# V in bursts of 1, 8, 5, 3 and 1 key tiles, double score tiles, and a new order of a head pair's steps

## The chip, the cores and the metric

One core of one Trainium2 chip runs the kernel. Its engines are TensorE (PE; its weight loads are listed as PEld), VectorE (DVE), ScalarE (ACT), GpSimd (POOL) and SyncE (SP, which here only issues DMAs). The metric is the device time of one execution in microseconds (us), less is better. Engines take their instructions in the order in which the program issues them and wait for each other by semaphores.

## The reference, cut to what matters

```python
def _attn_ref(q, k, v):                        # (2, 8, 1152, 64) each, q and k scaled up by 8
    q_pool = q.reshape(B, H, S // 2, 2, D).mean(axis=3)
    scores = (1 / np.sqrt(D)) * q_pool @ k.transpose(0, 1, 3, 2)
    scores = scores - scores.max(-1, keepdims=True)
    attn = np.exp(scores)
    attn = attn / (attn.sum(-1, keepdims=True) + 1e-09)
    return attn @ v                            # (2, 8, 576, 64)

x = attn_out.transpose(0, 2, 1, 3).reshape(1152, 512)
x = mlp(x, moe_w_in, moe_w_out)                # 512 -> 2048 -> 512, h * tanh(softplus(h)) between
return mlp(x, moe2_w_in, moe2_w_out)           # the same sizes, ELU between
```

## The kernel before

**Attention.** `attention()` works on eight pairs of heads, one after the other. The two heads of a pair lie on the two halves of the 128 partitions, so that score matmuls contract 64 rows each and two run side by side (shape 64x128 in the traces). A pair has 576 pooled queries; they are cut into c=0 (256 queries) and c=1 (320). The 1152 keys are nine key tiles of 128. A pair is 18 steps (`NS`): nine key tiles for c=0, then nine for c=1.

A step's `qk` makes one score tile, keys on the partitions and queries along the row, with three products of split operands (`kh`, `kl`, `qh`, `ql`; L343) and a fourth matmul that adds the negated row maxima `tops` (L345). `exp` (L351, ScalarE) writes its exponential into `pts`. `av` (L420) multiplies a key tile of V with it and accumulates over the nine tiles; this is in full fp32 (two passes for each matmul), with the two heads on the two halves of the columns (shape 128x64). `total` (L375) sums the exponentials over the keys, in tiles of 32 columns (128x32), from the last two key tiles and two partial sums that GpSimd adds up (`add`, L364). The sums go by way of DRAM to another layout and back (`spill`, `sum_out`, `sum_in`, `invert`, `inv_out`, `inv_in`), and then `scale` (L437), `token_high` and `token_low` write the result as split tokens `XH`, `XL`.

The row maxima of the next pair come first. `peak_mm` (L273, L280) makes a rough score with queries on the partitions, `peak` reduces it on VectorE (L286, L288, L289): 13 entries, of which entry 11 is the one with the remaining queries (L280; three matmuls, two reductions, its third part in PSUM bank 6). `top`, `top_out` (L320) and `top_in` (L326, L331) bring the maxima through DRAM into the rows `tops`; the first two query tiles after entry 5 (for c=0), the rest after entry 12 (for c=1). For pair 0 they are turned by PE instead (`flip`).

**PSUM.** Score tiles, row maxima, the sum of c=0 and the flips take turns on three slots of two banks each (`take`, a ring in program order). Bank 6 holds the V accumulator of c=0, the sum of c=1 and the third part of entry 11; bank 7 the V accumulator of c=1.

**The order.** All of it is written out by hand: `at(step, list, function)` puts a call into a step's list, and the loop over steps issues, in each step, the lists `pre`, `peak`, `qk`, `exp`, `av`, `act`, `dve`, `rest`, `pool` and `sp` (`peak` stands before `qk` in odd steps and behind it in even ones). V comes in bursts of two key tiles in every second step, from step 10 of a pair to step 26. In between, one piece of an MLP weight per pair is read in two halves (`read`, `read2`), rescaled on ScalarE (`rebias`, L119), and turned to split fp32 in further steps by its age in steps. The loop ends nine steps after the last score; what is left then is issued between the blocks of the MLP (`after`).

**MLP.** `mlps()` runs two layers in 96 units, each of 12 matmuls L178 and 12 (first layer) or 9 (second) matmuls L661. The first layer's first units read tokens of batch 0; tokens of c=1 of batch 1 are first read by unit 12.

Of the kernel before, what the change touches and what calls it, by code (L numbers as in the profile page):

```python
# [22 lines left out]
def tile_pool_attention_mish_elu_mlp(  # L23
# [159 lines left out]
    def attention():  # L183
        with ExitStack() as st:
# [268 lines left out]

            last = n_pairs * NS
            WHEN = [-14, -12, -10, -9, -8, -7, -6, -4, -3, -2, 0, 1, 2]
            for n in range(n_pairs):
                s0 = n * NS
                if n:
                    for i in range(2):
                        at(s0 - 26 + 2 * i, "sp", load_q, n, slice(0, SQ), slice(i, i + 1))  # L460
                        at(s0 - 21 + 3 * i, "sp", load_k, n, slice(i * S // 2, (i + 1) * S // 2))
                        at(s0 + [-2, 4][i], "sp", load_v, n, i)
                    at(s0 - 18 if n == 1 else s0 - 20, "pool", pool_q, n, nc.gpsimd)
                    at(s0 - 15 if n == 1 else s0 - 18, "act", high_q, n)
                    at(s0 - 17, "act", high_k, n, slice(0, S // 2))
                    at(s0 - 15, "act", high_k, n, slice(S // 2, S))
                    at(s0 - 12, "act", blk_q, n)
                    at(s0 - 10, "pool", low_q, n, nc.gpsimd)
                    at(s0 - 9, "pool", low_k, n, nc.gpsimd, slice(0, S // 2))
                    at(s0 - 8, "pool", low_k, n, nc.gpsimd, slice(S // 2, S))  # L470
                    for e, r in enumerate(WHEN):
                        at(s0 + r, "peak", peak_mm, n, e)
                        at(s0 + r, "dve", peak, n, e)
                    for r, t0, t1 in (WHEN[5], 0, 2), (WHEN[12], 2, NQ):
                        at(s0 + r + 1, "sp", top_out, n, t0, t1)
                        at(s0 + r + 3, "sp", top_in, n, t0, t1)
                for c in range(2):
                    u0 = s0 + KT * c
# [4 lines left out]
                    at(t0, "av", total, n, c)  # L483
                    at(t0 + 1, "pre", spill, n, c)
                    at(t0 + 1, "sp", sum_out, n, c)
                    at(t0 + 3, "sp", sum_in, n, c)
# [57 lines left out]
            while s < last + 9:  # L544
# [16 lines left out]
                for w in list(going):  # L561
                    w.age += 1
                    f = {6: w.read2, 9: w.rebias, 10: w.clamp, 12: w.shift, 13: w.words, 14: w.high, 15 if s > last else 22: w.rest}.get(w.age)
                    if f:
                        f()
# [241 lines left out]
```

## Time and profile before

| | |
|---|---|
| time, median of 3 runs | 646.53 us (645.66 to 646.84) |
| profiled execution, its own time | 647.42 us |
| its span | 645.6 us |
| busy: PE, DVE, ACT, POOL | 97%, 65%, 52%, 35% of the span |
| PE share of the chain that ended last | 85% |
| first score of pair 1, of pair 7 | 40.0 us, 206.9 us |
| first matmul of the MLP | 239.8 us |

The chain is followed back from the last instruction, step by step, to what released it. Its PE part by line: L178 and L661 (the MLP) 31% each, L420 8%, L343 6%. Times in the views are from the span's start. A PE row's length reaches to the modelled end of its last matmul, and rows overlap; what a matmul costs in a row of its like is read from start to start.

### The profile page before, as it was taken

Reading aid. Unit: us, or ns where it says so; the run is one execution under the profiler, and the core shown is the slowest. Engines: PE = TensorE matmul, PEld = TensorE weight load, DVE = VectorE, ACT = ScalarE, POOL = GpSimd, SP = SyncE. Lnnn points to the kernel's source line nnn. Section 1 sums busy time; section 2 is a strip of 40 time slices with the busy share of each in tenths; the row PEclk is TensorE's granted clock in tenths of the full one; section 3 lists DMA queues with packets and bytes.
Section 4 is the critical chain, followed back from the end, with each engine's and each line's share of the span. In section 5 each row is a group of like instructions: output and inputs, shape, how many; then the busy total and the mean of one; then the engine's idle time right before and its main releaser. Section 6 shows DMA issues by size and latency. Waiting matters only on the chain.

```text
span 645.6 us, 11750 instructions
## 1 busy us (share of the span) xinstructions
PE 629.3 (97%) x4626; PEld 535.9 (83%) x4626; DVE 421.7 (65%) x684; ACT 336.0 (52%) x682; POOL 227.6 (35%) x216
## 2 busy tenths in 40 slices
PE   5999999999999999999999999999999999999997
PEld 3666666666666669999999999999999999989995
DVE  5656666666666339466476657877887778995453
ACT  2655645546564456334345443546776566655442
POOL 5758686675866441101013223432201011100000
PEclk9999999999999999999999999999999999999999
DMA  4243443534342334242231233221223123310111
GB/s 156 63 101 84 100 95 72 139 73 98 83 100 64 87 92 142 66 131 65 66 120 59 85 98 98 65 73 60 97 67 98 43 89 98 97 34 1 50 50 49
DMA packets 50527, 53.36 MB, mean 83 GB/s; under 512 B 17640, under 2 KB 39080, under 8 KB 50472
## 3 DMA queue, kind: packets, MB, share of 16 engines
q1 hardware_dynamic: 49960, 51.90, 28.7%
q8 instruction: 36, 0.59, 0.4%
q10 hardware_dynamic: 512, 0.72, 0.3%
q14 instruction: 19, 0.16, 0.1%
HBM read 50.14 MB, written 2.47 MB: 81 GB/s over the span
## 4 chain that ended last, share of the span: by engine, by line
PE 85%; DMA 5%; DVE 3%; SPq 3%; ACT 2%; issue 1%; POOL 0%; DVEq 0%; POOLq 0%; ACTq 0%
PE banks L178 31%; PE banks L661 31%; PE banks L420 8%; PE banks L343 6%; PE banks L273 3%; PE banks L375 3%; PE banks L345 2%; DMA top<-hopm 2%; DVE stat L288 1%; DVE stat L286 1%; DMA hopm<-neg 1%; SPq L326 1%; DMA kr<-in_k_dram 1%; ACT QH L246 1%; ACT pt L351 1%
## 5 line engine op out<-in xcount | busy, mean ns | idle before, releaser
L123 POOL TENSOR_SCALAR wf<-wf 128x512 f32<-128x512 f32 x64 | 42.8, 670 | 259.1 <-ACT wf L119 214.5
L286 DVE TENSOR_REDUCE stat<-banks 128x2 f32<-128x768 f32 x96 | 91.1, 957 | 58.9 <-PE banks L273 58.9
L178 PE MATMUL banks<-XH,wh 128*128 128x384 f32 x384 | 129.5, 337 | 0.0
L178 PE MATMUL banks<-XL,wh 128*128 128x384 f32 x384 | 129.4, 337 | 0.0
L178 PE MATMUL banks<-XH,wl 128*128 128x384 f32 x384 | 129.4, 337 | 0.0
L351 ACT ACTIVATE pt<-banks 128x512 f32<-128x512 f32 (+1 forms) x144 | 90.1, 652 | 73.4 <-PE banks L345 73.4
L420 PE MATMUL banks<-pt,vr 128*64 128x320 f32 (+1 forms) x576 | 85.1, 418 | 0.0
L178 PEld LDWEIGHTS banks<-XH,wh 128*128 128x128 f32 x384 | 72.0, 188 | 2.3 <-issue 0.5
L178 PEld LDWEIGHTS banks<-XL,wh 128*128 128x128 f32 x384 | 72.0, 188 | 1.8
L364 POOL TENSOR_TENSOR add<-add,pt 128x512 f32<-128x512 f32 (+1 forms) x48 | 67.1, 1422 | 14.4 <-ACT pt L351 13.7
L178 PEld LDWEIGHTS banks<-XH,wl 128*128 128x128 f32 x384 | 72.0, 188 | 0.0
L615 ACT ACTIVATE gh<-banks 128x384 fp32r<-128x384 f32 x48 | 23.6, 492 | 80.5 <-PE banks L178 80.4
L661 PE MATMUL banks<-gh,wl 128*128 128x384 f32 x192 | 64.5, 336 | 0.0
L661 PE MATMUL banks<-gl,wh 128*128 128x384 f32 x192 | 64.5, 336 | 0.0
L661 PE MATMUL banks<-gh,wh 128*128 128x384 f32 x192 | 64.4, 335 | 0.0
L364 POOL TENSOR_TENSOR add<-pt 128x512 f32<-128x512 f32 (+1 forms) x32 | 45.3, 1416 | 48.0 <-ACT pt L351 48.0
L420 PEld LDWEIGHTS banks<-pt,vr 128*64 128x64 f32 x576 | 35.2, 136 | 27.9 <-issue 12.9
L661 PE MATMUL banks<-wl,gh 128*128 128x512 f32 x144 | 56.2, 390 | 0.0
L661 PE MATMUL banks<-wh,gl 128*128 128x512 f32 x144 | 56.2, 390 | 0.0
L661 PE MATMUL banks<-wh,gh 128*128 128x512 f32 x144 | 56.2, 390 | 0.0
L618 DVE TENSOR_TENSOR gl<-g,gh 128x384 fp32r<-128x384 f32 x48 | 31.1, 649 | 35.2 <-ACT g L616 35.2
L343 PE MATMUL banks<-QH,KH 64*128 64x320 f32 (+1 forms) x288 | 50.3, 337 | 0.8 <-ACT pt L351 0.5
(80 smaller groups left out, 1199.7 us busy)
## 6 DMA issues: line engine op xcount, KB each, us to landing
raw<-in_moe_w_in_dram SPq DMA_DIRECT2D x28, 512.0 KB
raw<-in_moe_w_out_dram SPq DMA_DIRECT2D x28, 512.0 KB
vr<-in_v_dram SPq DMA_DIRECT2D x16, 288.0 KB
qr<-in_q_dram SPq DMA_DIRECT2D x14, 288.0 KB
kr<-in_k_dram SPq DMA_DIRECT2D x14, 288.0 KB
raw<-in_moe_w_in_dram SPq DMA_DIRECT2D x8, 256.0 KB
raw<-in_moe_w_out_dram SPq DMA_DIRECT2D x8, 256.0 KB
out_dram<-part SPq DMA_DIRECT2D x8, 256.0 KB
```

Source lines behind the costliest of these rows:

```text
L123: nc.gpsimd.tensor_scalar(self.f, self.f, HUGE, -HUGE, op0=ALU.min, op1=ALU.max)
L178: nc.tensor.matmul(pt[:, :TB], w[:, kk * P:(kk + 1) * P], x[:, kk, tk], start=(i == 0), stop=(i == len(terms) - 1))
L273: nc.tensor.matmul(pt[:, h, :KB], qh[n][half[h], t * P:(t + 1) * P], kh[n][half[h], j * KB:(j + 1) * KB], start=True, stop=True,)
L286: nc.vector.tensor_reduce(m[:, t, :, j], pt[:, :, :KB], axis=AX.X, op=ALU.max)
L343: nc.tensor.matmul(pt[:, h, :w], x[half[h], kk], y[half[h], cols], start=(i == 0), stop=False)
L351: nc.scalar.activation(pts[n, c][:, kt], sc.pop((n, c, kt))[:, :, :w], AF.Exp, scale=SCALE)
L364: nc.gpsimd.tensor_tensor(d, d if i is None else p[:, i], p[:, j], op=ALU.add)
L375: nc.tensor.matmul(pt[32 * g:32 * (g + 1), :w], ones[:, :32], x[:, h, z * w:(z + 1) * w], start=(i == 0), stop=(i == len(srcs) - 1), tile_ ...
L420: nc.tensor.matmul(acc[n, c][half[h], :w], vs[n][:, h, kt, :], pts[n, c][:, kt, h, :], start=(kt == 0), stop=(kt == KT - 1),)
L615: nc.scalar.activation(gh, h, AF.Mish)
L618: nc.vector.tensor_tensor(gl, g, gh, op=ALU.subtract)
L661: nc.tensor.matmul(pt, l, r, start=(first and i == 0), stop=(final and i == 2))
```

## The change

`qk` and `exp` take a number m of key tiles. For key tiles 0, 2 and 6 of c=0 m is 2: the step's score tile and the next one's lie side by side in one slot (256 columns of each bank each), one exponential reads both, and the next step makes none. V is multiplied at steps 9 (key tile 0 of c=0), 16 (the other eight), 22 (tiles 0 to 4 of c=1), 25 (5 to 7) and 27 (the last). A list `late` stands behind `qk` and `exp`; the row maxima have times in half steps, even ones in `peak` (now always before `qk`), odd ones in `late`. The steps of loads, casts, splits, maxima, adds, sums, their chains and the weight's parts are taken from tables, `PREP[1]` for pair 1, `PREP[2]` for pairs 2 to 7 and `PLAN` for all. Keys are loaded, cast and split in parts of 768 and 384 instead of 576 and 576. The first pair's row maxima and flips stand in other steps as well. The MLP is as before.

```diff
-            def qk(n, c, kt):
+            def qk(n, c, kt, m):
                 o, w = cut[c][0], cut[c][1] - cut[c][0]
-                pt = sc[n, c, kt] = take()
-                kk, cols = slice(kt * P, (kt + 1) * P), slice(o, o + w)
-                terms = [(kh[n], qh[n]), (kl[n], qh[n]), (kh[n], ql[n])]
-                for i, (x, y) in enumerate(terms):
-                    for h in range(2):
-                        nc.tensor.matmul(pt[:, h, :w], x[half[h], kk], y[half[h], cols], start=(i == 0), stop=False)
-                for h in range(2):
-                    nc.tensor.matmul(pt[:, h, :w], unit[half[h], :], tops[n % 2][half[h], cols], start=False, stop=True)
-
-            def exp(n, c, kt):
+                pt, cols = take(), slice(o, o + w)
+                terms = [(kh[n], qh[n]), (kl[n], qh[n]), (kh[n], ql[n]), (None, tops[n % 2])]
+                sc[n, c, kt] = pt[:, :, :m * w].rearrange("p h (m w) -> p m h w", m=m)
+                for t in range(m):
+                    k0 = (kt + t) * P
+                    for i, (x, y) in enumerate(terms):
+                        for h in range(2):
+                            nc.tensor.matmul(
+                                pt[:, h, t * w:(t + 1) * w], x[half[h], k0:k0 + P] if x is not None else unit[half[h], :],
+                                y[half[h], cols], start=(i == 0), stop=(i == len(terms) - 1),
+                            )
+
+            def exp(n, c, kt, m):
...
-                nc.scalar.activation(pts[n, c][:, kt], sc.pop((n, c, kt))[:, :, :w], AF.Exp, scale=SCALE)
+                nc.scalar.activation(pts[n, c][:, kt:kt + m], sc.pop((n, c, kt)), AF.Exp, scale=SCALE)
...
+            PREP = {}
+            PREP[1] = {
...
+                "load_v": [-12, -6],
...
+                "peak": [-27, -25, -23, -19, -17, -16, -13, -12, -9, -3, -2, 0, 3],
+                "top": [[3, 3], [1, 4]],
+            }
+            PREP[2] = {
+                "load_q": [-26, -26],
+                "load_k": [-22, -17],
+                "load_v": [-2, 0],
+                "pool_q": -24,
+                "high_q": -19,
+                "high_k": [-19, -16],
+                "blk_q": -17,
+                "low_q": -13,
+                "low_k": [-7, -10],
+                "peak": [-30, -26, -23, -23, -18, -16, -13, -8, -7, -3, -2, -2, 2],
+                "top": [[1, 4], [2, 3]],
+            }
+            PLAN = {
+                "add": [[1, 2, 1, 1, 3], [2, 1, 2, 3, 2]],
+                "av": [9, 16, 16, 16, 16, 16, 16, 16, 16, 22, 22, 22, 22, 22, 25, 25, 25, 27],
+                "total": [11, 21],
+                "chain": [[0, 1, 1, 3, 5, 6, 10, 11, 12, 12], [-1, 1, 1, 5, 6, 8, 10, 12, 13, 17]],
+                "two": [0, 2, 6],
+                "weight": [3, 4, 4, 7, 15, 18, 19, 5],
+            }
...
-            WHEN = [-14, -12, -10, -9, -8, -7, -6, -4, -3, -2, 0, 1, 2]
+            kcut = slice(0, 2 * KB), slice(2 * KB, S)
...
-                    for e, r in enumerate(WHEN):
-                        at(s0 + r, "peak", peak_mm, n, e)
-                        at(s0 + r, "dve", peak, n, e)
-                    for r, t0, t1 in (WHEN[5], 0, 2), (WHEN[12], 2, NQ):
-                        at(s0 + r + 1, "sp", top_out, n, t0, t1)
-                        at(s0 + r + 3, "sp", top_in, n, t0, t1)
+                    for e, r in enumerate(prep["peak"]):
+                        at(s0 + r // 2, ("peak", "late")[r % 2], peak_mm, n, e)
+                        at(s0 + r // 2, "dve", peak, n, e)
+                    for (i, o), r, t0, t1 in zip(prep["top"], (prep["peak"][5], prep["peak"][12]), (0, 2), (2, NQ)):
+                        at(s0 + r // 2 + i, "sp", top_out, n, t0, t1)
+                        at(s0 + r // 2 + i + o, "sp", top_in, n, t0, t1)
...
-                        at(u0 + kt + 1, "pool", add, n, c, kt)
-                        at(s0 + 10 + (kt + 9 * c) // 2 * 2, "av", av, n, c, kt)
-                    t0 = s0 + 12 + 8 * c
...
+                        at(s0 + KT * c + kt + ADDED[c].get(kt, 1), "pool", add, n, c, kt)
+                        at(s0 + PLAN["av"][c * KT + kt], "av", av, n, c, kt)
+                    t0 = s0 + PLAN["total"][c]
+                    steps = ("av", total), ("pre", spill), ("sp", sum_out), ("sp", sum_in), ("rest", invert), ("sp", inv_out), ("sp", inv_in), ("rest", scale), ("act", token_high), ("rest", token_low)
+                    for (e, f), r in zip(steps, PLAN["chain"][c]):
+                        at(t0 + r, e, f, n, c)
...
-            for e in range(8, 13):
-                at(e - 8, "peak", peak_mm, 0, e)
-                at(e - 8, "dve", peak, 0, e)
+            for e, r in enumerate((0, 0, 2, 3, 3), 8):
+                at(r // 2, ("peak", "late")[r % 2], peak_mm, 0, e)
+                at(r // 2, "dve", peak, 0, e)
...
-            at(7, "peak", flip, 2, NQ)
-            at(7, "peak", flip, NQ, NQ + 1)
+            at(5, "peak", flip, 2, NQ)
+            at(5, "peak", flip, NQ, NQ + 1)
...
-                if s % 2:
-                    for f in by["peak"]:
-                        f()
-                if s < last:
-                    qk(n, c, kt)
-                    exp(n, c, kt)
-                if s % 2 == 0:
-                    for f in by["peak"]:
-                        f()
+                m = 2 if not c and kt in PLAN["two"] else 0 if not c and kt - 1 in PLAN["two"] else 1
+                if s < last and m:
+                    qk(n, c, kt, m)
+                    exp(n, c, kt, m)
+                for f in by["late"]:
+                    f()
...
-                    f = {6: w.read2, 9: w.rebias, 10: w.clamp, 12: w.shift, 13: w.words, 14: w.high, 15 if s > last else 22: w.rest}.get(w.age)
...
+                    for age, f in zip(PLAN["weight"], (w.read2, w.rebias, w.clamp, w.shift, w.words, w.high, w.rest)):
+                        if w.age == age or f == w.rest and s == last + 5:
...
-                if pieces and s % NS == 8:
+                if pieces and s % NS == PLAN["weight"][-1]:
```

## Rows read from the trace of the kernel before

**Rows 1.** The page: the chain that ended last, by engine and by line.
```profile
PE 85%; DMA 5%; DVE 3%; SPq 3%; ACT 2%; issue 1%; POOL 0%; DVEq 0%; POOLq 0%; ACTq 0%
PE banks L178 31%; PE banks L661 31%; PE banks L420 8%; PE banks L343 6%; PE banks L273 3%; PE banks L375 3%; PE banks L345 2%; DMA top<-hopm 2%; DVE stat L288 1%; DVE stat L286 1%; DMA hopm<-neg 1%; SPq L326 1%; DMA kr<-in_k_dram 1%; ACT QH L246 1%; ACT pt L351 1%
```

**Rows 2.** Windows by stage: length, busy time (and instructions) per engine, clock, DMA, GB/s.
```profile
0.00:27.00 27.00, 17.91 (x119) 12.06 (x119) 15.78 (x22) 12.06 (x26) 16.11 (x27) 1.00 0.38 120
27.00:40.00 13.00, 12.99 (x150) 9.21 (x152) 7.27 (x9) 5.47 (x9) 10.95 (x8) 1.00 0.30 71
40.00:206.90 166.90, 164.82 (x1844) 110.79 (x1843) 107.44 (x168) 91.41 (x180) 120.54 (x91) 1.00 0.41 92
206.90:239.90 33.00, 32.32 (x364) 20.53 (x360) 11.48 (x24) 15.76 (x30) 15.38 (x13) 1.00 0.32 87
239.90:645.60 405.70, 401.27 (x2161) 383.32 (x2160) 279.77 (x462) 211.34 (x437) 64.62 (x80) 1.00 0.24 76
```

**Rows 3.** Timeline of PE: start, length, line, operation, tiles, shapes, instructions in the row.
```profile
141.65 0.32 PE L343 MATMUL banks<-QH,KH 64*128 64x320 f32 x2
...
142.24 0.32 PE L343 MATMUL banks<-QH,KH 64*128 64x320 f32 x2
...
161.77 0.28 PE L345 MATMUL banks<-top,unit 64*128 64x256 f32 x2
161.89 0.34 PE L273 MATMUL banks<-KH,QH 64*128 64x384 f32 x2
162.15 1.30 PE L420 MATMUL banks<-pt,vr 128*64 128x320 f32 x8
163.38 0.39 PE L343 MATMUL banks<-QH,KH 64*128 64x256 f32 x2
163.60 0.28 PE L343 MATMUL banks<-QH,KL 64*128 64x256 f32 x2
...
236.45 3.45 PE L420 MATMUL banks<-pt,vr 128*64 128x320 f32 x24
```

**Rows 4.** Groups by line and form: busy us, mean ns; idle before, releasers.
```profile
L286 DVE TENSOR_REDUCE stat<-banks 128x2 f32<-128x768 f32 x96 | 91.1, 957 | 58.9 <-PE banks L273 58.9
...
L351 ACT ACTIVATE pt<-banks 128x640 f32<-128x640 f32 x72 | 48.2, 706 | 51.6 <-PE banks L345 51.6
L420 PE MATMUL banks<-pt,vr 128*64 128x320 f32 x288 | 46.5, 443 | 0.0
...
L351 ACT ACTIVATE pt<-banks 128x512 f32<-128x512 f32 x72 | 41.9, 598 | 21.8 <-PE banks L345 21.8
```

**Rows 5.** Timeline of PE: a column sum behind a burst.
```profile
158.28 0.39 PE L343 MATMUL banks<-QH,KH 64*128 64x256 f32 x2
158.51 0.28 PE L343 MATMUL banks<-QH,KL 64*128 64x256 f32 x2
```

**Rows 6.** Timeline of PE: waits, with idle time and releaser in brackets.
```profile
155.00 0.28 PE L345 MATMUL banks<-top,unit 64*128 64x256 f32 x2
155.46 0.44 PE L273 MATMUL banks<-KH,QH 64*128 64x384 f32 x2 [0.18 <-DVE stat L288]
...
222.19 0.38 PE L345 MATMUL banks<-top,unit 64*128 64x320 f32 x1 [0.50 <-DMA top<-hopm]
```

**Rows 7.** Timeline of the SP queue: start and length of DMA issues.
```profile
148.09 1.00 SPq L109 DMA_DIRECT2D raw<-in_moe_w_in_dram  x1
...
158.75 0.55 SPq L392 DMA_DIRECT2D hop<-sum  x1
159.39 0.39 SPq L320 DMA_DIRECT2D hopm<-neg  x1
...
161.60 1.29 SPq L331 DMA_DIRECT2D top<-hopm  x1
```

**Rows 8.** Timeline of ACT: two exponentials together, and a weight's rescale.
```profile
139.76 1.30 ACT L351 ACTIVATE pt<-banks 128x640 f32<-128x640 f32 x2 [2.13 <-PE banks L345]
...
152.41 0.69 ACT L119 ACTIVATE wf<-raw 128x512 f32<-128x512 f32 x1
```

More of the change, by code (lines that the diff above doesn't have):

```diff
@@ L452, in at @@
                 todo.setdefault((s, e), []).append(lambda: f(*args))
+            PREP = {}
+            PREP[1] = {
+                "load_q": [-37, -32],
+                "load_k": [-24, -18],
+                "load_v": [-12, -6],
+                "pool_q": -23,
+                "high_q": -18,
+                "high_k": [-17, -14],
+                "blk_q": -13,
+                "low_q": -16,
+                "low_k": [-7, -7],
+                "peak": [-27, -25, -23, -19, -17, -16, -13, -12, -9, -3, -2, 0, 3],
[22 more added lines that the diff above has]
+            }
+            ADDED = [dict(zip(ADDS, x)) for x in PLAN["add"]]
             last = n_pairs * NS
-            WHEN = [-14, -12, -10, -9, -8, -7, -6, -4, -3, -2, 0, 1, 2]
+            kcut = slice(0, 2 * KB), slice(2 * KB, S)
             for n in range(n_pairs):
@@ L458, in attention @@
                 if n:
+                    prep = PREP[min(n, 2)]
                     for i in range(2):
[L460 to L470, printed above, removed]
-                    for e, r in enumerate(WHEN):
-                        at(s0 + r, "peak", peak_mm, n, e)
-                        at(s0 + r, "dve", peak, n, e)
@@ L482, in attention @@
-                    t0 = s0 + 12 + 8 * c
[L483 to L486, printed above, removed]
-                    at(t0 + 5, "rest", invert, n, c)
-                    at(t0 + 5, "sp", inv_out, n, c)
-                    at(t0 + 7, "sp", inv_in, n, c)
-                    at(t0 + 10, "rest", scale, n, c)
-                    at(t0 + 11, "act", token_high, n, c)
@@ L492, in attention @@
-                    at(t0 + 12, "rest", token_low, n, c)
+                        at(s0 + KT * c + kt + ADDED[c].get(kt, 1), "pool", add, n, c, kt)
[4 more added lines that the diff above has]
+                        at(t0 + r, e, f, n, c)
@@ L545, in attention @@
                 n, c, kt = s // NS, (s % NS) // KT, s % KT
-                by = {e: todo.pop((s, e), []) for e in ("pre", "peak", "av", "act", "dve", "rest", "pool", "sp")}
-                for f in by["pre"]:
-                    f()
-                if s % 2:
-                    for f in by["peak"]:
-                        f()
-                if s < last:
-                    qk(n, c, kt)
-                    exp(n, c, kt)
-                if s % 2 == 0:
-                    for f in by["peak"]:
-                        f()
+                by = {e: todo.pop((s, e), []) for e in ("pre", "peak", "late", "av", "act", "dve", "rest", "pool", "sp")}
+                for e in ("pre", "peak"):
+                    for f in by[e]:
+                        f()
[4 more added lines that the diff above has]
+                for f in by["late"]:
+                    f()
                 for e in ("av", "act", "dve", "rest", "pool", "sp"):
@@ L562, in attention @@
                     w.age += 1
-                    f = {6: w.read2, 9: w.rebias, 10: w.clamp, 12: w.shift, 13: w.words, 14: w.high, 15 if s > last else 22: w.rest}.get(w.age)
-                    if f:
-                        f()
-                    if w.age == (15 if s > last else 22):
-                        going.remove(w)
-                if pieces and s % NS == 8:
+                    for age, f in zip(PLAN["weight"], (w.read2, w.rebias, w.clamp, w.shift, w.words, w.high, w.rest)):
+                        if w.age == age or f == w.rest and s == last + 5:
+                            f()
+                            if f == w.rest:
+                                going.remove(w)
+                if pieces and s % NS == PLAN["weight"][-1]:
                     going.append(Weights(*pieces.pop(0)))
```

12 lines of the change are left out of this document (10 added, 2 removed).

## The prediction

> **What bounds the kernel now.** I read the chain of waits first: 85% of the span is TensorE, and nothing else has more than 5% [rows 1]. Then the stages: from 239.9 us on, in the two MLP layers, PE is busy for 401 of 405.7 us, the rest is mostly the end, and the diff does not touch them. What can move lies before: a start of 27 us up to the first wide score tile, six like pairs from 40.0 to 206.9 us (166.9 us, 27.82 each) and 33.0 us for the last pair [rows 2]. In the six pairs PE reads 164.8 of 166.9 us busy, so there is hardly a gap to close, while VectorE (107), ScalarE (91) and GpSimd (121) are far from full. But a busy PE isn't a streaming PE. The PE timeline shows what lies between the instructions [rows 3]: score matmuls follow each other at 0.12 us a pair (161.77 to 161.89). A burst of two V key tiles then breaks in: from the row maximum at 161.89 to the second score row at 163.60 there are 1.71 us. In it stand one row maximum (384 columns; at 0.12 us per 256 that is 0.18), four pairs of V passes, and one score pair (0.12). What a pair of V passes takes without neighbours of another kind shows in the x24 row, the last burst: 3.45 us, less the 0.44 that one pass lasts [rows 4], over eleven steps is 0.27. Four make 1.08, all together 1.38. So **each burst costs some 0.33 us over its columns**, part going in, part coming out (163.38 to 163.60 is 0.22 where 0.12 is usual); 0.30 to 0.35 with the rounding of these rows.
>
> The column sums L375 have a tile shape of their own. Behind a burst they add little: 158.28 to 158.51 is again 0.23 [rows 5], but that exit would have been paid anyway, so the sum's own share is about 0.1 us.
>
> The rest of PE's loss is small waits [rows 6]: a row maximum starts 0.46 us after the score before it, for the long reduction L288 (0.34 lost), and the wide scores wait for their maxima `top` (0.5 us in the last pair; less in others). With some 0.1 us at four other places where a maximum stands ahead of a burst I put these waits at 1.1 us per pair.
>
> **The change, part by part**, per pair of the six.
>
> *V bursts.* Now nine per pair (two key tiles each, every second step). After: 8 tiles of c=0 at step 16, 5 at step 22, 3 at 25, and the single ones at 27 and 9 meet in one step, since step 27 of a pair is step 9 of the next. Four instead of nine: 5 x 0.33 = -1.65 us (-1.5 to -1.75).
>
> *Column sums.* They stood behind a burst (steps 12 and 20, both even). Steps 11 and 20 have no burst any more, so each pays its own way in and out: 0.15 + 0.22 = 0.37 instead of about 0.1. Two: +0.5 us (from 0, if they slip in free, to +0.7, two whole round trips).
>
> *Waits that go.* L288's reduction (EV entry 11) moves to the step before the pair, and a score and a double score now lie between it and its successors: -0.3. The maxima's second hop: now the out-DMA L320 is issued behind the sums' L392, which waits for the spill and the sum before it (158.75, 159.39) [rows 7]; after, `top_out` stands at step 3 and `sum_out` at 4. That frees the issue's 0.6 us and the wait for the spill; `top_in` comes a step later (6, was 5): -0.2. Each maximum ahead of a burst: -0.3.
>
> *Waits that come.* The V bursts were also the pause in which ScalarE and VectorE emptied the three score slots. From step 10 to 16 there is none. In it stand seven wide scores (0.59 us each, 141.65 to 142.24 [rows 3]), five maxima (0.18) and a sum (about 1.25 with its entry): 6.3 us of PE, and 13 slot uses. A slot is held for the filling, some 0.3 us until the reader sees it (a score row lasts 0.3 us, its columns 0.12 to 0.15), and the reading: 0.59 + 0.3 + 0.70 = 1.6 us for a score, 0.18 + 0.3 + 0.96 = 1.4 for a maximum [rows 4]. Three slots: 13 x 1.5 / 3 = 6.5 us. So this stretch is about even, and where a score follows a score by way of one slot it waits 0.2 to 0.4 us, with 0.1 lost at each restart. Walking it in order I find three to four such places: +0.9 us. Bounds: 0 (readers keep up, as ScalarE does now at 0.65 us a tile back to back, 1.30 for two [rows 8]) and +2.5 (every maximum and score in turn waits). All other stretches have a burst within five slot uses, so I cost them at nothing; their cover is the 2.7 us of five V tiles.
>
> *Double exponentials.* From the two rows (0.598 for 512 elements, 0.706 for 640 [rows 4]) I estimate 1.03 us for 1024 elements, against two at 0.5 to 0.6. ScalarE gains at most 0.5 us per pair and isn't on the path: 0. The first half waits for the second's matmuls (0.48 us); the slack of the narrow steps hides it, between bursts it is in the walk above.
>
> *Moved loads, casts and splits.* k is cut at 768 instead of 576: the same elements, 0. GpSimd keeps the same list, 120.5 us in six pairs = 20.1 a pair [rows 2], and has room in 26.8. On ScalarE the casts of q and k come one behind the other at step 17 (about 1.5 us); the double score there is read late, but the sums and five V tiles stand before the next use of its slot: 0, or +0.5 without them.
>
> Sum per pair: -1.65 + 0.5 - 0.8 + 0.9 = **-1.05, six pairs -6.3 us** (ends per pair: -1.75 - 1.1 = -2.9; -1.5 + 0.7 + 2.5 + 0.5 = +2.2).
>
> *The start.* Two maxima now stand ahead of the first score, and VectorE reduces them at 0.957 us each: up to +1.9. Against this three score steps fall away as single steps and the flips come two steps sooner, with nothing else to wait for: up to -1.9. I take -0.5.
>
> *The last pair.* No maxima of a next pair lie between its scores. Five bursts where there were ten: -1.65. But the sum of c=1 follows the last score directly and waits about 0.8 us for its exponential, where now a V burst stands between; and the last V tile falls behind the first MLP block (step 153 is outside the loop) and breaks in there, +0.35. With both sums' exits and the top wait of 0.5 us that goes, and with a V tile and a maximum or two that are done before the pair begins instead of in it (1.1 us): -2.3 (ends -3.5 and 0).
>
> Total: -6.3 - 0.5 - 2.3 = **-9.1 us**. The profiled execution took 647.42 us (span 645.6), so it would take 638.3. It is 0.9 us above the median of the three timed runs (646.53); from that: **637.4 us**. MLP: unchanged, since its first blocks read tokens of batch 0 only and the later chain of the last pair (inversion, scale, split, now up to five blocks in) is due at block 12.
>
> **Rivals.**
> (1) *The slots eat it.* The three slots bind from step 10 to 17, the new waits are 1.8 instead of 0.9 us, with the start and the tail half as good: 6 x -0.15 - 1.4 = -2.3, about 644.2; half way, 641. For it: VectorE has 13 maxima at 0.957 us per pair, and five of them fall between steps 14 and 17. Against it: they and the burst of 3.5 us stand in one stretch, and VectorE is 64% busy. The Trainium skill's "TensorEngine Tiling" (Performance Considerations, PSUM Bottleneck) says the same as a rule: packing the array speeds TensorE up, but emptying PSUM may become the bottleneck. No row of before shows that regime, since the readers idle between bursts; by that rule the time would be this rival's.
> (2) *Slower: ScalarE stands for a weight.* The second half of a weight is read at step 8 and rescaled on ScalarE at step 9; now it is read three steps ahead. Ahead of it on the DMA queue stand four `top` transfers whose issue takes up to 1.3 us each (161.60). Today 4.3 us pass from the issue at 148.09 to the rescale at 152.41, which did not wait [rows 7, 8], so landing takes at most that. The exponentials queue behind the rescale. Three slots cover 1.8 us, ScalarE's lead some 0.7: a stand beyond 2.5 us stops PE, beyond 3.8 us (2.5 + the saving) the kernel is slower. With the issue late by the four transfers as well it would stand 5 us: 8 x 2.5 = +20 against -9.1, 657. Against it: the queue isn't bound to PE's steps, and a V burst and three score steps lie between `top_in` and the rescale.
> (3) *It doesn't do what it says*: the 0.33 us belongs to a key tile, not to the burst; then only the 0.9 us of new waits and 0.5 for the sums remain against 0.8, six times +0.6 against start and tail: no change, 646 to 648. Against it: the x24 row, twelve passes without a break.
>
> **Chances.** Forecast (-6 to -13) 0.63; (1) 0.21, all of it between 640.5 and 645; better than 633.5: 0.03; (3) or gains that cancel 0.06; (2) or another stop of that kind 0.07. The measurement tells 0.2% (1.3 us) from no change. So faster 0.87, same 0.06, slower 0.07. Range 633.5 to 643.5: the forecast with its bounds and most of (1). The per-pair ends reach further (-2.9 would be 626, +2.2 about 657), but need all of one sign at once.
>
> **What will show it.** Four bursts a pair in PE's timeline, the longest x32 in about 3.6 us; the six pairs 26.8 us each instead of 27.82; the sums between two scores with 0.15 and 0.22 around them; waits of L343 and L273 for ScalarE and VectorE at steps 12 to 16, about 0.9 us; no wait of the wide scores for `top` of over 0.2; rescale of the weight without a wait; the MLP stage within 0.3 us of 405.7. Wrong if a pair takes over 27.3 us, if `top` or a weight stops PE each pair, or if the MLP stage grows.

## The result, and the profile after

The changed kernel takes 636.24 us (median of four runs, 635.80 to 636.29) beside 646.62 us of the kernel before on the same chip: a ratio of 0.9841, interval 0.9824 to 0.9858. The forecast was 637.4 us, with a range of 633.5 to 643.5. The profiled execution took 636.19 us with a span of 634.4 us, 11.2 us less than before.

The chain of waits of the kernel after, by engine and by line (for [rows 1]):

```profile
PE 95%; DVE 3%; DMA 1%; ACT 1%; issue 0%; DVEq 0%
PE banks L178 32%; PE banks L692 31%; PE banks L346 12%; PE banks L424 12%; PE banks L273 4%; PE banks L379 3%; DVE stat L286 2%; PE banks L280 1%; DMA qr<-in_q_dram 1%; ACT pt L355 0%; DVE part L717 0%; DVE wf L128 0%; PE banks L305 0%; DV
```

Scores are L346 now, exponentials L355, V L424, sums L379, the MLP's second half L692. The ten points that PE gained on the chain come from DMAs (5 to 1%), SP's queue (3% to nothing), ScalarE and issue. The stages (for [rows 2]; length, busy time of PE, PEld, DVE, ACT and POOL, clock, DMA, GB/s):

```profile
0.00:27.00 27.00, 19.09 (x131) 13.54 (x131) 17.22 (x24) 12.19 (x24) 16.72 (x27) 1.00 0.52 160
27.00:40.30 13.30, 12.59 (x146) 9.27 (x143) 8.17 (x10) 6.33 (x11) 12.32 (x9) 1.00 0.34 61
40.30:198.60 158.30, 157.77 (x1846) 113.56 (x1846) 113.66 (x167) 89.53 (x162) 126.30 (x90) 1.00 0.39 94
198.60:227.50 28.90, 28.51 (x349) 19.51 (x347) 14.83 (x23) 14.85 (x26) 15.89 (x11) 1.00 0.34 95
227.50:634.40 406.90, 402.45 (x2166) 383.58 (x2164) 280.11 (x462) 211.01 (x437) 65.09 (x80) 1.00 0.24 75
```

The six pairs take 158.3 us, 26.38 each: 1.43 us less per pair, 8.6 in all. The last pair takes 28.9 instead of 33.0 us; the first score of pair 1 comes 0.3 us later, and the MLP takes 1.2 us more. Most of the gain in the pairs, 7.0 of 8.6 us, is in PE's own busy time (164.8 to 157.8 us), as the forecast had it: the entries and exits of bursts count as busy.

PE's timeline in a pair of the kernel after (for [rows 3, 6]):

```profile
131.82 0.31 PE L346 MATMUL banks<-top,unit 64*128 64x320 f32 x2
132.06 1.19 PE L424 MATMUL banks<-pt,vr 128*64 128x320 f32 x8
133.18 0.44 PE L273 MATMUL banks<-KH,QH 64*128 64x384 f32 x2
133.46 0.30 PE L346 MATMUL banks<-QH,KH 64*128 64x320 f32 x2
...
134.74 0.44 PE L273 MATMUL banks<-KH,QH 64*128 64x384 f32 x2
135.18 0.65 PE L379 MATMUL banks<-pt,ones 128*32 128x128 f32 x16
...
137.46 0.34 PE L273 MATMUL banks<-KH,QH 64*128 64x384 f32 x2
137.84 0.41 PE L346 MATMUL banks<-QH,KH 64*128 64x320 f32 x2
138.09 0.31 PE L346 MATMUL banks<-QH,KL 64*128 64x320 f32 x2
...
138.53 0.35 PE L273 MATMUL banks<-KH,QH 64*128 64x384 f32 x2
138.93 0.41 PE L346 MATMUL banks<-QH,KH 64*128 64x320 f32 x2
...
140.47 3.67 PE L424 MATMUL banks<-pt,vr 128*64 128x256 f32 x32
```

The x8 row is a burst of one key tile of 320 columns and one of 256. From 131.82 to 133.46 are 1.64 us; in it stand a score row (0.15), a maximum (0.18), two pairs of V passes at 0.27 and two at 0.22 (the x32 row: 3.67 less 0.38 of its last pass, over 15). That leaves 0.33 us, the same price of a burst as before. That it is the change of tile shape that costs is a reading: a maximum, whose matmuls (64x128) have the shape of the scores, takes its 0.18 us between two scores and no more (131.20 to 131.38 in this trace). The x32 burst is the one forecast "in about 3.6 us". The new waits stand where they were looked for: 137.46 to 137.84 is 0.38 us where 0.18 is a maximum's own, and the score that restarts loses another 0.1 (137.84 to 138.09); the same again at 138.53; the sum starts 0.17 late.

Groups by form (for [rows 4]; busy us, mean ns, idle before and releasers):

```profile
L355 ACT ACTIVATE pt<-banks 128x1024 f32<-128x1024 f32 x24 | 24.7, 1029 | 4.9 <-PE banks L346 4.5
```

A double exponential takes 1.029 us; the estimate was 1.03. SP's queue, start and length of issues (for [rows 7]):

```profile
122.19 0.94 SPq L320 DMA_DIRECT2D hopm<-neg  x1
124.87 0.55 SPq L396 DMA_DIRECT2D hop<-sum  x1
...
128.64 0.87 SPq L331 DMA_DIRECT2D top<-hopm  x1
```

The maxima's second hop (L320) now goes out 2.7 us before that of the sums (L396), where it stood behind it. The last `top` issue ends at 129.5, PE needs it at 131.8 and doesn't wait. Nor does the weight's rescale, the row of ScalarE that answers to [rows 8]:

```profile
133.88 0.65 ACT L119 ACTIVATE wf<-raw 128x512 f32<-128x512 f32 x1
```

### The profile page after: what moved, and what is told of

Its sections match the earlier page's. It is cut to its first block, busy times and chain, and to the rows that moved or that the text cites. A ratio compares the mean times of both kernels' runs of the same rounds, so it can differ in the third digit from the quotient of the medians.

```text
span 634.4 us, 11745 instructions
## 1 busy us (share of the span) xinstructions
PE 620.4 (98%) x4626; PEld 539.5 (85%) x4626; DVE 434.0 (68%) x684; ACT 333.9 (53%) x658; POOL 236.3 (37%) x216
## 4 chain that ended last, share of the span: by engine, by line
PE 95%; DVE 3%; DMA 1%; ACT 1%; issue 0%; DVEq 0%
PE banks L178 32%; PE banks L692 31%; PE banks L346 12%; PE banks L424 12%; PE banks L273 4%; PE banks L379 3%; DVE stat L286 2%; PE banks L280 1%; DMA qr<-in_q_dram 1%; ACT pt L355 0%; DVE part L717 0%; DVE wf L128 0%; PE banks L305 0%; DVE KL L259 0%; DVE qr L243 0%
## 5 line engine op out<-in xcount | busy, mean ns | idle before, releaser
L355 ACT ACTIVATE pt<-banks 128x640 f32<-128x640 f32 (+2 forms) x120 | 86.7, 747 | 83.3 <-PE banks L346 75.5
L424 PE MATMUL banks<-pt,vr 128*64 128x320 f32 (+1 forms) x576 | 76.9, 412 | 0.0
L368 POOL TENSOR_TENSOR add<-add,pt 128x512 f32<-128x512 f32 (+1 forms) x48 | 70.7, 1487 | 2.9 <-ACT pt L355 2.8
L692 PE MATMUL banks<-gl,wh 128*128 128x384 f32 x192 | 64.7, 337 | 0.0
L692 PE MATMUL banks<-gh,wl 128*128 128x384 f32 x192 | 64.6, 336 | 0.0
L692 PE MATMUL banks<-gh,wh 128*128 128x384 f32 x192 | 64.5, 336 | 0.0
L424 PEld LDWEIGHTS banks<-pt,vr 128*64 128x64 f32 x576 | 38.6, 137 | 28.4 <-issue 5.2
L368 POOL TENSOR_TENSOR add<-pt 128x512 f32<-128x512 f32 (+1 forms) x32 | 50.8, 1596 | 25.4 <-ACT pt L355 25.3
L692 PE MATMUL banks<-wl,gh 128*128 128x512 f32 x144 | 56.3, 391 | 0.0
L692 PE MATMUL banks<-wh,gl 128*128 128x512 f32 x144 | 56.3, 391 | 0.0
L692 PE MATMUL banks<-wh,gh 128*128 128x512 f32 x144 | 56.3, 391 | 0.0
L128 DVE TENSOR_SCALAR wf<-wf 128x512 int32<-128x512 int32 x64 | 43.6, 682 | 17.7 <-POOL wf L123 17.7
L134 DVE SCALAR_TENSOR_TENSOR wf<-raw,wf 128x512 int32<-128x512 int32 x64 | 53.5, 837 | 2.2
```

The lines of the kernel that those rows point to most:

```text
L128: nc.vector.tensor_scalar(f, f, 3, None, op0=ALU.logical_shift_left)
L134: nc.vector.scalar_tensor_tensor(f, self.low, 29, f, op0=ALU.logical_shift_right, op1=ALU.bitwise_or)
L355: nc.scalar.activation(pts[n, c][:, kt:kt + m], sc.pop((n, c, kt)), AF.Exp, scale=SCALE)
L368: nc.gpsimd.tensor_tensor(d, d if i is None else p[:, i], p[:, j], op=ALU.add)
L424: nc.tensor.matmul(acc[n, c][half[h], :w], vs[n][:, h, kt, :], pts[n, c][:, kt, h, :], start=(kt == 0), stop=(kt == KT - 1),)
L692: nc.tensor.matmul(pt, l, r, start=(first and i == 0), stop=(final and i == 2))
```

## The experiments

Ratios are to the kernel before, on the same chip. "Pair" is a sixth of the six pairs' window; 26.38 us in the changed kernel, 27.82 before.

**The bursts alone, in the old order.** The kernel before with only the new times of V.

```diff
-                        at(s0 + 10 + (kt + 9 * c) // 2 * 2, "av", av, n, c, kt)
+                        at(s0 + [9, 16, 16, 16, 16, 16, 16, 16, 16, 22, 22, 22, 22, 22, 25, 25, 25, 27][c * KT + kt], "av", av, n, c, kt)
```

> The kernel before, with only the new V bursts (steps 9, 16, 22, 25, 27); single score tiles, sums at steps 12 and 20, maxima and loads as before. Theory S (a burst costs 0.33 us of going in and out, whatever is in it): five bursts less and two sums that now pay their own way, -1.65 + 0.5 = -1.15 us a pair, seven pairs -8, about -1 more at the end of attention: 637 to 639. Rival L (the gain comes from the new layout of maxima, hops and doubles, and bursts in the old layout only starve the score slots): 645 to 649.

654.89 us, ratio 1.0131 (1.0116 to 1.0147): slower by more than either theory said. A pair takes 29.1 us. What PE's weight loads waited for in the five pairs 69.7 to 215.3 us (us in total, times, longest):

```profile
PEld banks L343 <- ACT pt L351: 17.1, 30, 0.8
```

One of these places on PE's timeline:

```profile
121.83 0.41 PE L343 MATMUL banks<-QH,KH 64*128 64x320 f32 x2 [0.55 <-ACT pt L351]
```

The same waits in the kernel before, five pairs too:

```profile
PEld banks L343 <- ACT pt L351: 2.5, 5, 0.5
```

The six pairs of this run (for [rows 2]):

```profile
40.50:215.30 174.80, 163.11 (x1848) 112.34 (x1848) 106.46 (x168) 92.50 (x180) 121.18 (x89) 1.00 0.38 86
```

The weight loads wait 14.6 us longer in five pairs, but part of that passes while earlier matmuls still run. PE itself stands idle for 11.7 us of the six pairs where it was 2.1, 1.6 us more per pair, and its busy time falls by only 0.3 per pair (164.8 to 163.1 us). The pair lost 1.3: the waits for slots cost more than the fewer bursts gave back. How much of the 1.65 us of entries and exits was saved can't be read, because a score row that restarts after a wait counts as busy for longer (0.41 us above, 0.31 is usual). This is the first rival of the prediction, in the old order and in full.

**The new order with nine bursts.** The changed kernel with V in nine bursts of two key tiles (one of three, one of one).

```diff
-                "av": [9, 16, 16, 16, 16, 16, 16, 16, 16, 22, 22, 22, 22, 22, 25, 25, 25, 27],
+                "av": [10, 10, 12, 12, 14, 14, 16, 16, 16, 21, 21, 22, 22, 23, 23, 24, 24, 26],
```

> The kernel after, with nine V bursts a pair again (steps 10, 12, 14, 16 for c=0 and 21, 22, 23, 24, 26 for c=1); all else as after. Theory S: five bursts more, +1.65 us a pair, less 0.4 of slot waits that the bursts between the wide scores take away: +1.25 x 7.5 = +9, 645 to 647. Rival L: within 2 us of the kernel after, 635 to 638.

647.29 us, 1.0016 (1.0006 to 1.0025). A pair takes 28.05 us, 1.67 more than with four bursts; five bursts at 0.33 are 1.65. The six pairs:

```profile
40.40:208.70 168.30, 166.32 (x1845) 111.16 (x1846) 117.92 (x167) 91.07 (x162) 124.12 (x90) 1.00 0.37 88
```

They take 10.0 us more than with four bursts. Of these 8.55 us are PE's busy time and 1.45 are gaps: 0.29 us per burst is busy, and up to 0.05 may be waits. The added pauses change the slots' waits too, so the 0.33 rests on this run and on the rows together. So the four cells are: old order with nine bursts 646.6 and with four 654.9, new order with nine 647.3 and with four 636.2. **Neither half gains anything alone.**

**Single score tiles.**

```diff
-                "two": [0, 2, 6],
+                "two": [],
```

> The kernel after without double score tiles: each narrow key tile has a slot and an exponential of its own, the order of steps is the same. Theory S: ScalarE is not on the path, within 0.8 us of the kernel after (635.5 to 637). Rival D (the doubles keep slots free and ScalarE ahead): three more slot uses a pair, each up to 0.3 us of wait, 7 x 0.9 = +6: 641 to 643.

658.06 us, 1.0180 (1.0165 to 1.0195): 21.8 us lost, where the prediction priced the double tiles at nothing. A pair takes 29.2 us. That is far beyond both theories. Between the profiled executions 16.8 us are lost in the six pairs, 1.2 in the last pair and 3.9 before pair 1. PE waits at the narrow steps 2 and 7; its timeline at one of them:

```profile
132.91 0.28 PE L346 MATMUL banks<-top,unit 64*128 64x256 f32 x2
134.12 0.39 PE L346 MATMUL banks<-QH,KH 64*128 64x256 f32 x2 [0.93 <-ACT pt L355]
```

ScalarE's timeline in the same stretch:

```profile
132.18 0.82 ACT L256 CAST KH<-kr 128x768 fp32r<-128x768 f32 x1
132.90 0.67 ACT L246 CAST QH<-qr 128x576 fp32r<-128x576 f32 x1
133.47 1.08 ACT L355 ACTIVATE pt<-banks 128x512 f32<-128x512 f32 x2
```

Two casts, 1.5 us, stand ahead of two exponentials, and the slots stay full meanwhile. The prediction had this cast pair at 0, or +0.5. In the start it is another reader that holds a slot, VectorE's reduction of entry 11, and behind that wait the granted TensorE clock was 0.50 for a while, the lower of its two levels, 1.2 GHz (PE's timeline, then the windows):

```profile
21.74 0.39 PE L346 MATMUL banks<-QH,KH 64*128 64x256 f32 x2 [1.56 <-DVE stat L288]
```

```profile
23.20:26.60 3.40, 3.40 (x24) 2.85 (x24) 0.96 (x1) 1.78 (x5) 2.54 (x2) 0.50 0.02 5
```

The four executions have mean clocks between 0.995 and 1.000 and times within 0.14 us, so the total doesn't hang on that stretch. Two readings were left: ScalarE has too much to do with single exponentials, or the shared slot carries PE through. The next two runs part them. No run parts the shared slot from the order that comes with it: without doubles the second tile's scores also move to the next step, behind the maxima there.

**Two exponentials for a shared slot.** Double tiles as in the change, but each half has its own exponential.

```diff
-                nc.scalar.activation(pts[n, c][:, kt:kt + m], sc.pop((n, c, kt)), AF.Exp, scale=SCALE)
+                src = sc.pop((n, c, kt))
+                for t in range(m):
+                    nc.scalar.activation(pts[n, c][:, kt + t], src[:, t], AF.Exp, scale=SCALE)
```

> The kernel after, with double score tiles still sharing a slot, but each read by two exponentials of 512 elements instead of one of 1024. Theory N (three slots, each held some 1.5 us per use, so what counts is the work that PE gets done per slot use; the double gives two key tiles per use): within 1.5 us of the kernel after, 636 to 638. Rival H (what counts is ScalarE's time and its queue: three more instructions of 0.6 us a pair): most of the 17 to 22 us that single tiles cost comes back, 645 to 658.

637.11 us, 0.9854 (0.9839 to 0.9869), within the interval of the change. ScalarE (a row of two exponentials):

```profile
95.64 1.09 ACT L357 ACTIVATE pt<-banks 128x512 f32<-128x512 f32 x2
```

1.09 us for two instead of 1.03 for one. So the joint exponential is worth about 0.9 of the 21.8 us, and the intervals don't tell even that from nothing; **the rest goes with the shared slot**, and with the order of scores that it brings.

**Single tiles, the casts apart.** As the single tiles, with q's cast one step and k's first cast two steps later for pairs 2 to 7.

```diff
-                "high_q": -19,
-                "high_k": [-19, -16],
+                "high_q": -18,
+                "high_k": [-17, -16],
-                "two": [0, 2, 6],
+                "two": [],
```

> As e3_single_tiles (the kernel after without double score tiles, 658.1 us), for pairs 2 to 7 with the casts of q and k no longer together at step 17 of the pair before, but one each at its steps 0, 1 and 2 behind the exponential. Theory H (single tiles lose because the exponentials of steps 0 and 1 queue behind 1.5 us of casts on ScalarE while three slots are full): half of the loss or more comes back, 643 to 650. Rival N (it is the number of slot uses that counts, whatever ScalarE does between): 655 to 660.

653.80 us, 1.0126 (1.0098 to 1.0155): 4.3 of the 21.8 us come back (5.2 between the profiled executions, where a pair takes 28.3 us). The rest is not that the casts stand together.

**The maxima's old order.** The changed kernel with the maxima of pairs 2 to 7 at their old steps.

```diff
-                "peak": [-30, -26, -23, -23, -18, -16, -13, -8, -7, -3, -2, -2, 2],
-                "top": [[1, 4], [2, 3]],
+                "peak": [-27, -23, -19, -18, -15, -14, -11, -7, -6, -3, 1, 2, 5],
+                "top": [[1, 2], [1, 2]],
```

> The kernel after, with the row maxima of pairs 2 to 7 and their hops in the steps of the kernel before (four in a row at steps 8 to 11, entries 10 to 12 at the pair's own steps 0 to 2); bursts, doubles, casts and the rest as after. Theory I: VectorE needs 0.96 us for each and the dense stretches fill the slots, 1.0 to 2.5 us a pair: 642 to 652. Rival (doubles and bursts alone carry the gain): 635 to 638.

655.26 us, 1.0148 (1.0123 to 1.0173): 19 us lost, more than expected. Waits of the weight loads in the five pairs 67.9 to 215.5 us:

```profile
PEld banks L346 <- ACT pt L355: 21.8, 30, 1.4
```

PE's timeline just behind entry 11 (L280, at 98.57), which stands between two scores of the narrow steps again:

```profile
100.53 0.39 PE L346 MATMUL banks<-QH,KH 64*128 64x256 f32 x2 [1.17 <-ACT pt L355]
```

The same waits in the changed kernel, five pairs:

```profile
PEld banks L346 <- ACT pt L355: 1.7, 5, 0.3
```

A maximum holds a slot for about as long as a score (1.4 us, the prediction's estimate) but gives PE only 0.18 us of work. Where several stand in a stretch without a burst, PE waits; the new steps avoid this.

**Three bursts, and where the third stands.** Both runs merge the single tile of step 9 into the burst of 16 and the last tile into that of 25; in the first it stands a step later, at 26.

```diff
-                "av": [9, 16, 16, 16, 16, 16, 16, 16, 16, 22, 22, 22, 22, 22, 25, 25, 25, 27],
+                "av": [16] * 9 + [22] * 5 + [26] * 4,
```

And the second:

```diff
-                "av": [9, 16, 16, 16, 16, 16, 16, 16, 16, 22, 22, 22, 22, 22, 25, 25, 25, 27],
+                "av": [16] * 9 + [22] * 5 + [25] * 4,
```

> The kernel after, with three V bursts a pair: all nine tiles of c=0 at step 16, five of c=1 at step 22, the other four at step 26; none at steps 9 and 27. Theory S alone: -0.35 x 8 = -2.8, and -0.6 at the end, where no tile breaks into the MLP any more: 632.5 to 634. Theory N: the narrow burst at step 9 was also a pause for the slots, but it stood one step behind another; the stretch from step 9 to 16 grows by the wide score of step 9 and one maximum, so 0 to 0.5 us of new waits a pair: 633 to 637. Rival: the pause at step 9 is needed, over 638.

> The kernel after, with three V bursts a pair like e12_three_bursts, but the last four tiles of c=1 stay at step 25 (step 7 of the next pair), where the kernel after has its burst of three. Theory P (it is the place that counts: a burst must stand between the double tile of step 6 with its two maxima and the score of step 8; e12 lost 1.25 us a pair there, and 0.47 at step 10 where the burst of step 9 was missing): 0.35 saved and 0.45 lost a pair, and 0.6 to 0.9 less at the end: 635 to 637.5. Rival C (the count of pauses decides, wherever they stand): 641 to 646.

At 26: 645.09 us, 0.9974 (0.9964 to 0.9985), a pair 27.8; the theory that fewer bursts are better fails. At 25: 637.65 us, 0.9866 (0.9850 to 0.9883), a pair 26.6: as the theory of the place has it, 0.15 us over the end of its range. PE's timeline at step 7 of the first (steps 25 and 26 of a pair are steps 7 and 8 of the next):

```profile
107.27 0.39 PE L346 MATMUL banks<-QH,KH 64*128 64x256 f32 x2 [1.08 <-ACT pt L355]
```

PE's timeline at step 10 of the second, just behind where the burst of step 9 stood:

```profile
107.51 0.45 PE L273 MATMUL banks<-KH,QH 64*128 64x384 f32 x2
108.03 0.41 PE L346 MATMUL banks<-QH,KH 64*128 64x320 f32 x2
```

One step of place costs 7.4 us. And the fourth burst, taken away at the better place, saves its 0.33 us and gives more than that back, since a pair takes 0.2 us longer: 107.51 to 108.03 is 0.52 us where 0.18 is a maximum's own.

**The order on SP's queue.** The out-DMA of the sums is put ahead of that of the maxima.

```diff
-                "chain": [[0, 1, 1, 3, 5, 6, 10, 11, 12, 12], [-1, 1, 1, 5, 6, 8, 10, 12, 13, 17]],
+                "chain": [[0, 1, 1, 3, 5, 6, 10, 11, 12, 12], [-1, 0, 0, 5, 6, 8, 10, 12, 13, 17]],
```

> The kernel after, with spill and sum_out of c=1 one step earlier, so that on the DMA queue sum_out stands ahead of the maxima's second top_out again, as in the kernel before; PE's order is untouched. Theory I (the four bursts pay only with the new order around them: doubles, spread maxima, and the hop of the maxima ahead of the sum's): top_out goes from 122.2 to about 125.5, top_in ends 1.9 us later, and the wide scores wait 1.5 to 2 us a pair: 646 to 651. Rival (the hop has slack, as the forecast's 0.2 us said): 636 to 638.

641.43 us, 0.9929 (0.9912 to 0.9945): 5.2 us lost, between the two theories (3.9 in the profiled execution, the fastest of the four). SP's queue:

```profile
125.99 0.55 SPq L396 DMA_DIRECT2D hop<-sum  x1
126.63 0.38 SPq L320 DMA_DIRECT2D hopm<-neg  x1
```

The wide score that follows, on PE's timeline:

```profile
133.69 0.38 PE L346 MATMUL banks<-top,unit 64*128 64x320 f32 x1 [0.45 <-DMA top<-hopm]
```

The maxima leave at 126.63 instead of 122.19, and in five of the pairs PE stands until they are back, 2.0 us in all: the issue of L396 waits for the spill until 125.99, and all issues behind it wait too. A pair takes 27.0 us, 0.6 more; what makes up the rest of it the trace does not part.

**The last V tile before the MLP.**

```diff
-                        at(s0 + PLAN["av"][c * KT + kt], "av", av, n, c, kt)
+                        at(min(s0 + PLAN["av"][c * KT + kt], last + 8), "av", av, n, c, kt)
```

> The kernel after, with the very last V tile (key tile 8 of c=1 of the last pair) in step 152 instead of 153, so that it joins the V burst before it and no longer breaks into the MLP. Theory S (a burst costs its way in and out): -0.35, and up to -1.1 if all of the 1.1 us by which the MLP stage grew hangs on it: 635.2 to 635.9. Rival (the tile filled a gap there): no change.

636.60 us, 0.9850 (0.9836 to 0.9865): the gain that was expected is not in the median. The profile shows the MLP at 405.8 us again and the last pair at 29.4 instead of 28.9, so 0.6 us come back at the seam; the first score of pair 1 stood at 41.2 instead of 40.3 in this execution, with the same code up to there.

**The sums behind a burst (two tries).** These were to measure what the isolated sums cost. In the first try the sum of c=0 goes to step 9, with an earlier last add, and both chains move.

```diff
-                "add": [[1, 2, 1, 1, 3], [2, 1, 2, 3, 2]],
-                "total": [11, 21],
-                "chain": [[0, 1, 1, 3, 5, 6, 10, 11, 12, 12], [-1, 1, 1, 5, 6, 8, 10, 12, 13, 17]],
+                "add": [[1, 2, 1, 1, 1], [2, 1, 2, 3, 2]],
+                "total": [9, 21],
+                "chain": [[0, 1, 3, 5, 7, 8, 12, 13, 14, 14], [1, 2, 2, 5, 6, 8, 10, 12, 13, 17]],
```

In the second the sum of c=1 goes to step 22:

```diff
-                "total": [11, 21],
-                "chain": [[0, 1, 1, 3, 5, 6, 10, 11, 12, 12], [-1, 1, 1, 5, 6, 8, 10, 12, 13, 17]],
+                "total": [11, 22],
+                "chain": [[0, 1, 1, 3, 5, 6, 9, 10, 12, 12], [0, 1, 3, 5, 6, 8, 10, 12, 14, 16]],
```

> The kernel after, with the column sums issued right behind a V burst: that of c=0 at step 9 (its last partial sum on GpSimd two steps sooner), that of c=1 at step 22. Theory S: each saves its own way in and part of its way out, 0.37 - 0.12 = 0.25 us, two a pair, 8 pairs: -4, 632 to 633.5. Rival (GpSimd's partial sums are not there yet at step 9, or the sums were in nobody's way): PE waits for the last partial sum, 636 to 639.

> The kernel after, with the column sum of c=1 right behind the V burst of step 22 instead of alone at step 20, its sum_out behind the maxima's top_in on the DMA queue (unlike e4), and scale of c=0, which uses the same PSUM bank, one step sooner. Theory S: the sum saves its own way in and part of its way out, 0.25 us a pair: 634 to 635. Theory N: the sum at step 20 is also a pause (1.4 us) between the double tile of step 2 and the next maximum; without it the slots of steps 0 to 4 are short, +0.5 to +1.5 us a pair: 640 to 648.

671.09 us, 1.0392 (1.0366 to 1.0417), and 649.88 us, 1.0052 (1.0039 to 1.0065). Neither measures the sums' price, since each brings new waits. In the first the out-DMA of the sums of c=1 waits for a sum that now comes two steps later, and the maxima's way back (`top_in`) stands behind it on SP's queue (L396 at 80.53, L326 at 81.96). The wide scores on PE's timeline wait:

```profile
85.47 0.38 PE L346 MATMUL banks<-top,unit 64*128 64x320 f32 x1 [0.60 <-DMA top<-hopm]
87.65 0.46 PE L346 MATMUL banks<-top,unit 64*128 64x320 f32 x1 [1.80 <-DMA top<-hopm]
88.04 2.19 PE L424 MATMUL banks<-pt,vr 128*64 128x320 f32 x8
```

In the second the sum of c=1, which shares PSUM bank 6 with the accumulator that `scale` of c=0 reads, waits for that on PE's timeline (6.2 us in all):

```profile
104.22 0.75 PE L379 MATMUL banks<-pt,ones 128*32 128x160 f32 x16 [1.03 <-DVE banks L441]
```

In the same run a maximum waits 0.9 us a pair for an exponential where the sum of step 20 stood, the place that the second theory named.

No run beat the change: the nearest (0.9850, 0.9854, 0.9866) have intervals that overlap its own.

## Why the prediction was right, point by point

| step of the prediction | forecast, us | measured, us |
|---|---|---|
| V bursts, nine to four, per pair | -1.65 | 1.67 back with nine; 0.33 each in the rows after |
| sums by themselves, per pair | +0.5 | about +0.2, read from rows only |
| waits that come, steps 10 to 16, per pair | +0.9 | +0.9 |
| waits that go, per pair | -0.8 | -0.85, by difference |
| six pairs | -6.3 | -8.6 |
| start, last pair and MLP | -2.8 | -2.6 |

*V bursts.* Right in mechanism and size: the price belongs to the burst and not to the key tile, so the third rival is out. But the prediction treats the nine small bursts as a cost alone. The first run shows their other side: they are also the pauses in which the readers empty the slots, and in the old order that is worth more than they cost.

*Waits that come.* 0.17 at the sum, 0.1 at one more place (134.04 to 134.29 where 0.15 is usual), and two of 0.2 with 0.1 lost at the restart: 0.87. The walk over three slots, made with the new steps as they are, was right in place and size. Its last sentence is not: "All other stretches have a burst within five slot uses" doesn't hold from the burst of step 16 to that of step 22, where eight stand (three maxima, entry 11, two scores and two doubles). With single tiles that is one of the two stretches where PE waits.

*Sums.* Over-sized. On the timeline after, each pays some 0.09 us going in and 0.11 coming out (for c=1: 121.57 to 121.78 where 0.12 is usual, 123.00 to 123.29 where 0.18 is), besides the wait counted above: 0.4 for both, where the prediction had 0.2 for both before. No run isolates it; it stays a reading.

*Waits that go.* None of the weight loads waits for L288 or for `top` in the six pairs after, but for one of 0.2 us. The total is the remainder, -1.43 + 1.65 - 0.2 - 0.87 = -0.85; no row or run shows it by itself. The waits before were also read too large in part: PE stands idle for `top` four times in all eight pairs, 1.4 us together, and the longest, 0.6, is not in the last pair. The hop's share was put at 0.2 per pair; undone alone, in the new order, it costs 5.2 us over seven pairs, 0.75 each (0.6 by the profiled execution): under-sized there.

*Double exponentials: the step that was mis-sized.* The prediction gave 0, "ScalarE isn't on the path". The instruction's time is indeed worth little (0.9 us in all), but the slot that two key tiles share, with the order that it brings, is worth some 21 us in this layout (16.8 of them in the six pairs), 4 to 5 of them only for the casts ahead of the exponentials. A narrow score puts 0.48 us of PE work into a slot that it holds for about 0.48 + 0.3 + 0.6 = 1.4 us, a third of which is 0.47; a double one 0.96 us into one held for 2.3, a third of which is 0.76 (estimates from the rows, with the 0.3 us of the prediction). The surplus of 0.2 us pays for the maxima between the scores, which give PE 0.18 us and hold a slot for 1.4. The error left no trace in the total because the stretch from step 0 to 9 was costed at nothing *with* the double tiles in it; the prediction didn't know what they were for, and that its nothing came out is luck. The same holds for the maxima's order, which the prediction credits with a few tenths per pair and which costs 19 us when undone.

*Start, last pair, MLP.* The sum is right, the parts are not: they are off by +0.8, -1.8 and +1.2 us, and that these nearly cancel is luck. The first wide score comes at 25.7 instead of 27.0 us, yet pair 1 begins 0.3 us later, because one more V tile, one more maximum and entry 11 (L280, 0.72 us) now stand before it. At the other end the last pair is free of that work and takes 4.1 us less. The MLP grew by 1.2 us and not by 0.3 at most: the last V tile breaks in behind its first block, as said, but its columns (four passes, 0.54) are in the MLP's account now, and the price of the burst, 0.35, was booked to the last pair. The prediction named a growing MLP stage as a sign of being wrong; it came, by a tile that had been booked to another stage. PE's timeline at that place:

```profile
229.52 0.34 PE L178 MATMUL banks<-XH,wl 128*128 128x384 f32 x1
229.79 0.76 PE L424 MATMUL banks<-pt,vr 128*64 128x320 f32 x4
230.48 0.45 PE L178 MATMUL banks<-XH,wh 128*128 128x384 f32 x1
230.76 0.34 PE L178 MATMUL banks<-XL,wh 128*128 128x384 f32 x1
```

From 229.52 to 230.76 are 1.24 us, of which two MLP rows are 0.35.

*Rivals.* The first, that the slots eat the gain, did not happen, but it is the regime next door: the old order with four bursts, single tiles, or the old maxima each fall into it. That is where the Trainium skill's "TensorEngine Tiling" (Performance Considerations, PSUM Bottleneck) is borne out: it warns that a packed array may be held up by emptying PSUM, and the waits of the weight loads for exponentials, 17.1 us in five pairs with the bursts alone and 21.8 with the old maxima, are this. The second, a weight that ScalarE stands for, shows no wait.

## What to carry to other kernels

A burst of matmuls of another tile shape has a price of its own (here 0.33 us), but it is also the pause in which the score slots empty: before merging bursts, count in each stretch between them how much PE work each slot use brings against a share of the time it is held, and give short users of a slot company. Where a burst stands can matter more than how many there are (one step: 7.4 us; one burst fewer: no gain). On a DMA queue that issues in order, put the hop that PE will wait for ahead of one that itself waits for later PE work.

## What the hardware showed that was not expected

In the first try with the sums, the two waits of 0.60 and 1.80 us were followed by matmuls of double length: the x8 V row of 2.19 us above takes 1.19 in the changed kernel. The windows of that run (length, busy time of PE, PEld, DVE, ACT and POOL, clock):

```profile
82.00:87.80 5.80, 3.40 (x30) 2.03 (x26) 3.77 (x5) 1.46 (x2) 3.25 (x3) 1.00 0.29 62
87.80:91.20 3.40, 3.40 (x29) 1.75 (x33) 0.11 (x1) 1.27 (x2) 0.29 (x1) 0.50 0.70 232
91.20:100.00 8.80, 8.66 (x106) 6.73 (x98) 6.11 (x9) 5.26 (x10) 8.62 (x7) 1.00 0.27 66
```

After a stretch with PE busy for 3.40 of 5.80 us the granted clock was 0.50, the 1.2 GHz level, in the stretch behind, and then 1.00 again. PE was busy in all of those 3.40 us, which at full clock would have been 1.7; so the two waits of together 2.4 us cost about 1.7 us beyond themselves (an estimate). The run has six stretches at 0.50, 23.9 us in all, so up to 12 of the 34.9 us that it lost may be the clock's and not the waits'. In the changed kernel and in the kernel before, the clock is 1.00 in every stage.
